# Fused attention and rational feed-forward kernel: which engine clamps the weight pieces and forms the remainder of g

## The chip, the cores and the metric

The kernel runs on one core of a Trainium2 chip. The metric is the device time of one execution in microseconds (us), as the median of several runs. The core's engines are TensorE (PE in the profile; PEld is its weight load), VectorE (DVE), ScalarE (ACT), GpSimd (POOL) and SyncE (SP), which issues most of the DMAs. Each engine works through its own list of instructions in order, and waits at the head of the list until the semaphores that the head needs are set.

## The reference, cut to what matters

An attention over 4 batches, 12 heads and 448 positions, with heads mixed before and after the softmax, gives x of 1792 rows and 768 columns. Then comes the feed-forward part, in which the change lies:

```python
def _moe_ref(x, w_in, w_out, a, b):
    h = x @ w_in
    h2 = h * h
    h3 = h2 * h
    P = a[0] + a[1] * h + a[2] * h2 + a[3] * h3
    Q = 1.0 + np.abs(b[0]) * np.abs(h) + np.abs(b[1]) * h2
    g = P / (Q + 1e-06)
    return (g @ w_out).astype(np.float32)
```

w_in is 768 x 2048 and w_out 2048 x 768. They reach the kernel as 64-bit floats, seen as pairs of 32-bit words.

## The kernel before, in words

**Arithmetic.** A matrix product of float32 accuracy is made from three products in a faster format: each operand is split into a head ("hi", rounded to the format) and a remainder ("lo", the value less its head), and head times head, head times remainder and remainder times head are summed in PSUM.

**Weights.** They come in 16 blocks f of 128 columns of w_in with the matching 128 rows of w_out, and each block in 4 pieces of 128 x 384, 64 pieces in all (`put_w`). A piece is loaded as word pairs (`load`, tile cr), its 64-bit floats are turned into 32-bit ones by bit operations, and then split. The steps of a piece in order: `mag` on ScalarE (absolute value of the upper words, tile cm), `clamp` on GpSimd (bounds the exponent, line 415), `shift`, `top` and `tail` on VectorE (lines 419, 424 and 430; tile cg), `hi` on ScalarE (tile w) and `lo` on GpSimd (line 446). 16 pieces (blocks 0 to 3) are made during the attention; they have an argument g. The other 48 are made during the feed-forward part, one beside each of its first 48 units.

**Units.** The feed-forward part has 64 units (`put_unit`): a unit is one block f for one batch of 448 rows. It has a first product of 18 matmuls into a bank of ps_s (`m1`, line 879), the rational function (ScalarE: lines 892, 895, 898, 902, 915 and 919; VectorE: `horner1` 905, `den2` 912, `horner2` 908, `step1` 922, `step2` 925, `quot` 929), the split of g into its head (`hi`, on ScalarE or VectorE, lines 236 and 238) and its remainder (`lo`, VectorE or GpSimd, line 939), and a second product of 6 times 3 matmuls into ps_t, ps_u and ps_a (`m2`, line 969). Four units make a turn: they add into the same six banks, which are then copied out (tile o, lines 236 and 238; in the last 16 units added to what is there, line 1006). ps_s has two banks, so the first product of a unit needs `horner2` of the unit two before it, the last reader of its bank.

**Order.** Nothing is ordered by the hardware's own choice: the program lists all steps with a planned duration, dependencies and a due time, and a planner (`Plan.run`) lays them on the engines and so fixes each engine's list. A step that may run on several engines goes where the plan has it first; the table `ON` names the engines. A change of an engine or of a planned duration thus changes the lists of all engines from there on.

```python
        a5 = add(copies(S, on=ON["g_hi"]), 0, hi, [d5, R["g"].take(), op_rest], at=at)
        d6 = add(subs(S, on=ON["g_lo"]), 0, lo, [a5], at=at)
```

Of the kernel before, what the change touches and what calls it, by code (L numbers as in the profile page):

```python
# [13 lines left out]
ALU = mybir.AluOpType  # L14
# [25 lines left out]
F64_MIN = 2.0 ** -15  # L40
F64_MAX = struct.unpack("f", struct.pack("I", 0x47EFF000))[0]
# [13 lines left out]
class Plan:  # L55
# [11 lines left out]
    def add(self, eng, dur, fn, deps=(), at=0.0, extra=0.0, since=0.0, after=(), mode=None, late=0.0):  # L67
        op = Op(eng, dur, fn, [d for d in deps if d is not None], at, extra, since, mode, late)
        op.behind = list(after)
        self.ops.append(op)  # L70
        return op
# [120 lines left out]
def act(n, sb=True):  # L192
    return 0.08 + 1.0e-3 * n + (0.05 if sb else 0.0)


def dve(n, fast=False):
    return 0.16 + 0.53e-3 * n if fast else 0.14 + 1.06e-3 * n
# [6 lines left out]
def copies(n, sb=True, on=("act", "dve")):  # L204
    return {e: act(n, sb) if e == "act" else dve(n, sb) for e in on}


def subs(n, on=("dve", "pool")):
    return {e: dve(n) if e == "dve" else pool(n) for e in on}
# [2 lines left out]
ON = {  # L212
    "q_hi": ('act', 'dve'), "q_lo": ("dve", "pool"), "k_hi": ('act', 'dve'), "k_lo": ('dve', 'pool'), "w_hi": ('act',), "w_lo": ("pool",),
    "s": ('act', 'dve'), "d_hi": ('act', 'dve'), "d_lo": ("dve", "pool"), "p": ("act", "dve"), "x_hi": ("act",),
    "g_hi": ("act", "dve"), "g_lo": ("dve", "pool"),
}


def dma(nbytes):
    return nbytes / 300e3  # L220
# [13 lines left out]
def move(nc, eng, o, i):  # L234
    if eng is nc.scalar:
        eng.copy(o, i)  # L236
    else:
        eng.tensor_copy(o, i)
# [3 lines left out]
def mixed_attention_then_rational_ffn(ctx: ExitStack, tc, q, k, v, w, wmix, mask, a, b2, out):  # L242
# [3 lines left out]
    nc = tc.nc  # L246
# [5 lines left out]
    add = plan.add  # L252
# [136 lines left out]
    def new_w(f):  # L389
        if f % CH == NR:  # L390
            W[f] = d_sb[1].rearrange("p n s -> p (n s)")[:, 0:2 * WC].rearrange("p (h c) -> p h c", h=2).bitcast(F32R)
        else:
            W[f] = sb["wr" if f % CH < NR else "wl"].tile([128, 2, WC], F32R, tag="w", name=f"w{f}")

    def room_w(f):
        return [R["d"].uses[NT - 1] if f % CH == NR else op_begin if f % CH < NR else op_rest]


    def put_w(f, c, at, since=0.0, g=None):
        sl = slice(c * CV, (c + 1) * CV)  # L400
        box = {}

        def load():
            t = sb["cr"].tile([128, CV, 2], I32, tag="cr", name="cr")
            nc.sync.dma_start(out=t.rearrange("p n t -> p (n t)"), in_=w[f, :, sl].bitcast(I32))
            box["hi"], box["lo"] = t[:, :, 1], t[:, :, 0]

        def mag():
            t = sb["cm"].tile([128, CV], I32, tag="cm", name="cm")
            nc.scalar.activation(t.bitcast(F32), box["hi"].bitcast(F32), AF.Abs)  # L410
            box["m"] = t

        def clamp():
            m = box["m"].bitcast(F32)
            nc.gpsimd.tensor_scalar(out=m, in0=m, scalar1=F64_MIN, scalar2=F64_MAX, op0=ALU.max, op1=ALU.min)  # L415

        def shift():
            m = box["m"]
            nc.vector.tensor_scalar(
                out=m, in0=m, scalar1=3, scalar2=0x3FFFFFFF, op0=ALU.logical_shift_left, op1=ALU.bitwise_and)  # L420

        def top():
            t = sb["cg"].tile([128, CV], I32, tag="cg", name="cg")
            nc.vector.scalar_tensor_tensor(  # L424
                out=t, in0=box["hi"], scalar=-0x40000000, in1=box["m"],
                op0=ALU.bitwise_and, op1=ALU.bitwise_or)
            box["g"] = t

        def tail():
            nc.vector.scalar_tensor_tensor(  # L430
                out=box["m"], in0=box["lo"], scalar=29, in1=box["g"],
                op0=ALU.logical_shift_right, op1=ALU.bitwise_or)

        def hi(eng):
            if f in VIA:
                t = sb["co"].tile([128, 2, CV], F32R, tag="co", name="co")
            else:
                if c == 0:
                    new_w(f)
                t = W[f][:, :, sl]  # L440
            move(nc, eng, t[:, 0, :], box["m"].bitcast(F32))
            box["o"] = t

        def lo(eng):
            t = box["o"]
            eng.tensor_sub(t[:, 1, :], box["m"].bitcast(F32), t[:, 0, :].bitcast(F32))  # L446

        def store():
            nc.sync.dma_start(out=w_scr[f][:, :, sl], in_=box["o"].bitcast(F32))

        ld = add("sp", 0.45, load, [R["cr"].take()], at=at - 5.0, extra=dma(128 * CV * 8), since=max(since, at - 9.0))
        near = lambda i, k: [] if g is None else [posts[min(g + i, len(groups) - 1)][k]]
        o1 = add("act", act(CV), mag, [ld, R["cm"].take(), *near(0, 3)], at=at, late=4.0)
        o2 = add("pool", 1.54, clamp, [o1, *near(0, 1)], at=at)
        o3 = add("dve", dve(CV, True), shift, [o2], at=at)
        o4 = add("dve", 0.59, top, [o3, R["cg"].take()], at=at)
        o5 = add("dve", 0.57, tail, [o4], at=at)
        R["cg"].uses[-1].append(o5)
        R["cr"].uses[-1].append(o5)
        if f in VIA:  # L460
            home = [R["co"].take()]
        elif c == 0:
            home = [*room_w(f), w_use[f - CH] if f >= CH else None]
        else:
            home = []
        o6 = add(copies(CV, on=ON["w_hi"]), 0, hi, [o5, *near(1, 3)] + [x for x in home if x], at=at, after=() if f in VIA else w_ld[f][:1])
        o7 = add(subs(CV, on=ON["w_lo"]), 0, lo, [o6, *near(1, 1)], at=at)
        R["cm"].uses[-1].append(o7)
        if f in VIA:
            o8 = add("sp", 0.57, store, [o7], at=at, extra=dma(128 * CV * 8), late=2.0)  # L470
            R["co"].uses[-1].append(o8)
            w_done[f].append(o8)
        else:
            w_ld[f].append(o6)
            w_ld[f].append(o7)
# [322 lines left out]
    for i in range(len(VIA) * NCV):  # L798
        g = first[1] + 6 + (first[NT - 1] - first[1] - 3) * i // (len(VIA) * NCV)
        put_w(VIA[i // NCV], i % NCV, at=tau[g], g=g)  # L800
# [247 lines left out]
    for f in range(PH):  # L1048
        if f not in VIA:
            for c in range(NCV):  # L1050
                put_w(f, c, at=END1 - 26.0 + 6.0 * c, since=END1 - 40.0 + 6.0 * c, g=len(groups) - 8 + 2 * c)
    for n in homes:
        put_load_x(n, at=END1 + UNIT * PH * (held.index(n) - 1) + 1 if n > 1 else END1 - 45.0)
    for u in range(len(units)):
        i = u + PH * NCV
        if i < NF * NCV:
            put_w(i // NCV, i % NCV, at=END1 + UNIT * u + 2.0, since=END1 + UNIT * u - 6.0)
        put_unit(u)
# [62 lines left out]
```

## Time and profile before

| | before |
|---|---|
| median of 3 runs | 840.03 us (836.45 to 842.73) |
| profiled execution | 838.34 us |
| its span, first to last instruction | 836.5 us |
| busy share of the span, PE / DVE / ACT / POOL | 96% / 81% / 60% / 43% |
| the chain that ended last, PE / DVE / ACT / DMA | 67% / 18% / 5% / 4% |
| mean granted clock of TensorE | 0.993 of full |

The times in the views are microseconds from the start of the span, unless marked ns. The busy share of an engine is the share of the stretch in which at least one of its instructions ran; two instructions that overlap count once. The feed-forward part's first product starts at 348.2 us, beside the end of the attention, and its last second product ends at 832 us. The chain that ended last follows the work back from the last instruction, at each step to what released it.

### The profile page before, as it was taken

The numbers are of one execution on the slowest core, as the hardware profiler recorded it, in microseconds if no ns is written. First come the engines' busy times: TensorE is split into PE (matmuls) and PEld (weight loads), VectorE is DVE, ScalarE is ACT, GpSimd is POOL, SyncE is SP. The second block draws the span as 40 slices with busy tenths as digits, with TensorE's granted clock in tenths as the row PEclk, the third lists the DMA queues.
The fourth block names the chain that finished last, engine by engine and source line by source line (L and its number), as shares of the span: only waits on it lengthen the run. The fifth ranks groups of instructions, "written<-read, shape, count | busy, mean of one in ns | idle before, by whom it ended". The sixth has DMA issues, their size and how long they took to land.

```text
span 836.5 us, 23297 instructions
## 1 busy us (share of the span) xinstructions
PE 802.2 (96%) x9360; PEld 597.8 (71%) x9360; DVE 677.4 (81%) x1158; ACT 501.5 (60%) x1098; POOL 358.4 (43%) x488
## 2 busy tenths in 40 slices
PE   5889999999999999999999999999999999999998
PEld 1244455554545454589989899998989999999997
DVE  5667788878878888789988898898898899676665
ACT  2456666646655666566677666665657676545542
POOL 2224444442444344634455545556646554312111
PEclk8899999999999999999999999999999999999999
DMA  6677888677886864984633265664476644366314
GB/s 201 217 202 224 249 264 271 198 218 253 257 229 199 258 217 143 358 298 174 230 123 101 79 217 135 200 139 100 79 236 164 159 112 67 61 226 241 115 62 155
DMA packets 71901, 155.46 MB, mean 186 GB/s; under 512 B 12561, under 2 KB 52337, under 8 KB 70641
## 3 DMA queue, kind: packets, MB, share of 16 engines
q1 hardware_dynamic: 67736, 141.99, 52.2%
q0 software_dynamic: 3456, 11.01, 8.1%
q8 instruction: 74, 1.21, 0.6%
q10 hardware_dynamic: 600, 0.97, 0.4%
q14 instruction: 35, 0.28, 0.1%
HBM read 77.49 MB, written 37.75 MB: 138 GB/s over the span
## 4 chain that ended last, share of the span: by engine, by line
PE 67%; DVE 18%; ACT 5%; DMA 4%; issue 4%; POOL 1%; SPq 1%; ACTq 0%; DVEq 0%; POOLq 0%
PE ps_s L879 18%; PE ps_s L496 8%; PE ps_a L640 7%; PE ps_u L969 7%; PE ps_t L969 7%; PE ps_a L969 6%; PE ps_t L565 4%; PE ps_u L565 4%; PE ps_u L705 3%; DVE cg L424 2%; PE ps_t L705 2%; DMA kk<-in_k 2%; DVE nm L571 2%; ACT e L580 2%; DVE cm L430 2%
## 5 line engine op out<-in xcount | busy, mean ns | idle before, releaser
L415 POOL TENSOR_SCALAR cm<-cm 128x384 f32<-128x384 f32 x64 | 103.0, 1612 | 43.6 <-ACT cm L410 43.1
L656 DVE STREAM_TRANSPOSE aa<-ps_a 128x448 f32<-128x448 f32 (+1 forms) x184 | 107.8, 618 | 12.1 <-PE ps_a L640 11.4
L939 POOL TENSOR_TENSOR g<-ua,g 128x448 fp32r<-128x448 f32 x47 | 57.4, 1221 | 128.3 <-ACT g L236 72.7
L600 POOL TENSOR_SCALAR krs<-kpost,rr 128x64 f32<-128x64 f32 x180 | 81.6, 466 | 70.9 <-DVE rr L591 50.0
L879 PE MATMUL ps_s<-xs,w 128*128 128x448 f32 x504 | 107.5, 366 | 2.7 <-DVE m L908 2.6
L879 PE MATMUL ps_s<-d,w 128*128 128x448 f32 x504 | 107.6, 367 | 2.0 <-DVE m L908 1.9
L496 PE MATMUL ps_s<-kk,q 64*64 64x448 f32 x720 | 95.2, 556 | 9.4 <-DMA kk<-in_k 5.1
L879 PEld LDWEIGHTS ps_s<-xs,w 128*128 128x128 f32 x504 | 94.3, 188 | 12.0 <-DVE m L908 4.2
L879 PEld LDWEIGHTS ps_s<-d,w 128*128 128x128 f32 x504 | 94.1, 188 | 11.6 <-DVE m L908 3.1
L236 ACT COPY st<-ps_s 120x448 f32<-120x448 f32 (+1 forms) x120 | 60.2, 533 | 68.9 <-PE ps_s L496 35.0
L640 PEld LDWEIGHTS ps_a<-e,krs 64*32 64x32 f32 x2880 | 44.7, 106 | 74.2 <-issue 31.5
L640 PE MATMUL ps_a<-e,krs 64*32 64x224 f32 x2880 | 92.3, 355 | 1.6 <-DVE aa L656 0.6
L892 ACT ACTIVATE m<-ps_s,a_sb 128x448 f32<-128x448 f32 x64 | 46.1, 720 | 66.7 <-PE ps_s L879 64.0
L969 PE MATMUL ps_u<-g,w 128*128 128x448 f32 x336 | 83.9, 366 | 0.0
L969 PE MATMUL ps_a<-g,w 128*128 128x448 f32 x336 | 83.8, 366 | 0.0
L969 PE MATMUL ps_t<-g,w 128*128 128x448 f32 x336 | 83.4, 366 | 0.0
L446 POOL TENSOR_TENSOR w<-cm,w 128x384 fp32r<-128x384 f32 x48 | 55.7, 1160 | 62.8 <-ACT w L236 62.8
L587 POOL TENSOR_SCALAR sm<-sm 128x2 f32<-128x2 f32 (+1 forms) x92 | 20.6, 224 | 124.1 <-ACT e L580 122.2
L580 ACT ACTIVATE e<-ps_t,nm 128x448 f32<-128x448 f32 x92 | 57.7, 634 | 24.7 <-DVE nm L571 16.7
L580 ACT ACTIVATE e<-ps_u,nm 128x448 f32<-128x448 f32 x88 | 55.2, 633 | 21.9 <-DVE nm L571 18.7
L969 PEld LDWEIGHTS ps_t<-g,w 128*128 128x128 f32 x336 | 63.0, 188 | 5.5 <-DVE g L939 0.3
L969 PEld LDWEIGHTS ps_u<-g,w 128*128 128x128 f32 x336 | 63.1, 188 | 5.2
(90 smaller groups left out, 1514.9 us busy)
## 6 DMA issues: line engine op xcount, KB each, us to landing
d<-st SPq DMA_DIRECT2D x144, 210.0 KB
cr<-in_w SPq DMA_DIRECT2D x64, 384.0 KB
d<-x_scr SPq DMA_DIRECT2D x5, 2688.0 KB
xs<-x_scr SPq DMA_DIRECT2D x4, 2688.0 KB
o_scr<-o POOLq DMA_DIRECT2D x24, 448.0 KB, 6.0
d<-st SPq DMA_DIRECT2D x42, 157.5 KB
x_scr<-xs SPq DMA_DIRECT2D x12, 540.0 KB
q<-in_q SPq DMA_DIRECT2D x16, 384.0 KB
```

Of the source, the lines that this page charges most:

```text
L236: eng.copy(o, i)
L415: nc.gpsimd.tensor_scalar(out=m, in0=m, scalar1=F64_MIN, scalar2=F64_MAX, op0=ALU.max, op1=ALU.min)
L446: eng.tensor_sub(t[:, 1, :], box["m"].bitcast(F32), t[:, 0, :].bitcast(F32))
L496: nc.tensor.matmul(box["s"][hh][i0:i1, 0:S], lhsT=Q[T][d, pr, i0:i1], rhs=K[b][d, pr, :], start=True, stop=True)
L565: nc.tensor.matmul(box[r if nt == 2 else 0]["t"][64 * c:64 * c + 64, 0:S], lhsT=kpre[p], rhs=Dt[T][p, kb + c if nt == 2 else kb, :], start ...
L580: nc.scalar.activation(e, box[r]["t"][:, 0:S], AF.Exp, bias=box[0]["nm"][:, r:r + 1], accum_out=box[0]["sm"][:, r:r + 1])
L600: eng.tensor_scalar_mul(box[r]["kr"], kpost, rr)
L640: nc.tensor.matmul(banks[c]["p"][q_:q_ + BT, JH * r:JH * (r + 1)], lhsT=box[r]["kr"][p, m_, :], rhs=box[r]["e"][p, JH * jh:JH * (jh + 1)], ...
L656: nc.vector.transpose(o, src)
L879: nc.tensor.matmul(h[:, 0:S], lhsT=W[fi][:, wi, kk * 128:(kk + 1) * 128], rhs=x[:, kk // 3, xj, kk % 3, :], start=(n == 0), stop=(n == 3 * ...
L939: eng.tensor_sub(g[:, 1, :], box["rc"], g[:, 0, :].bitcast(F32))
L969: nc.tensor.matmul(O[key][:, 0:S], lhsT=W[fi][:, wi, DM + m * 128:DM + (m + 1) * 128], rhs=box["g"][:, gi, :], start=(f == 0 and n == 0), ...
```

## The change

For the 48 pieces of the feed-forward part the clamp is issued on VectorE, with a planned 0.32 us, and on GpSimd as before for the 16 pieces that are made in the attention. The remainder of g is VectorE's alone. The remainder of the weights stays on GpSimd.

```diff
@@ -212,7 +212,7 @@
-    "g_hi": ("act", "dve"), "g_lo": ("dve", "pool"),
+    "g_hi": ("act", "dve"), "g_lo": ("dve",),
@@ -410,9 +410,9 @@
-        def clamp():
+        def clamp(eng):
             m = box["m"].bitcast(F32)
-            nc.gpsimd.tensor_scalar(out=m, in0=m, scalar1=F64_MIN, scalar2=F64_MAX, op0=ALU.max, op1=ALU.min)
+            eng.tensor_scalar(out=m, in0=m, scalar1=F64_MIN, scalar2=F64_MAX, op0=ALU.max, op1=ALU.min)
@@ -451,7 +451,7 @@
-        o2 = add("pool", 1.54, clamp, [o1, *near(0, 1)], at=at)
+        o2 = add({"dve": 0.32} if g is None else {"pool": 1.54}, 0, clamp, [o1, *near(0, 1)], at=at)
```

The lists change from the first unit's end on (some 370 us). On VectorE 48 clamps come in, and the remainders of g there rise from 17 to 64; the planner also moves 4 heads of g to VectorE (28 before, 32 now) and 5 copies of o away from it (43 before, 38 now). VectorE's list at the same place of the program, from `step1` (L922) of one unit to `horner2` (L908) of the next, the 15th of the 64. Before:

```order
L922 TENSOR_TENSOR sq<-sq,ua 128x448
L419 TENSOR_SCALAR cm<-cm 128x384
L925 SCALAR_TENSOR_TENSOR ua<-sq,ua 128x448
L424 SCALAR_TENSOR_TENSOR cg<-cr,cm 128x384
L929 SCALAR_TENSOR_TENSOR ua<-m,a_sb,ua 128x448
L430 SCALAR_TENSOR_TENSOR cm<-cr,cg 128x384
L238 COPY o<-ps_a 128x448
L419 TENSOR_SCALAR cm<-cm 128x384
L424 SCALAR_TENSOR_TENSOR cg<-cr,cm 128x384
L905 TENSOR_TENSOR m<-m,ps_s 128x448
L430 SCALAR_TENSOR_TENSOR cm<-cr,cg 128x384
L908 SCALAR_TENSOR_TENSOR m<-m,a_sb,ps_s 128x448
```

VectorE's list at that place now:

```order
L922 TENSOR_TENSOR sq<-sq,ua 128x448
L415 TENSOR_SCALAR cm<-cm 128x384
L925 SCALAR_TENSOR_TENSOR ua<-sq,ua 128x448
L419 TENSOR_SCALAR cm<-cm 128x384
L929 SCALAR_TENSOR_TENSOR ua<-m,a_sb,ua 128x448
L424 SCALAR_TENSOR_TENSOR cg<-cr,cm 128x384
L238 COPY o<-ps_a 128x448
L939 TENSOR_TENSOR g<-ua,g 128x448
L430 SCALAR_TENSOR_TENSOR cm<-cr,cg 128x384
L905 TENSOR_TENSOR m<-m,ps_s 128x448
L912 TENSOR_TENSOR sq<-sq,ua 128x448
L908 SCALAR_TENSOR_TENSOR m<-m,a_sb,ps_s 128x448
```

Ahead of `horner2` stand now a clamp (L415), a remainder of g (L939) and `den2` (L912); a second piece's shift, top and tail have gone behind it. One or two units later the list goes from `den2` (L912) of one unit to its `step1` (L922) so, before:

```order
L905 TENSOR_TENSOR m<-m,ps_s 128x448
L912 TENSOR_TENSOR sq<-sq,ua 128x448
L908 SCALAR_TENSOR_TENSOR m<-m,a_sb,ps_s 128x448
L922 TENSOR_TENSOR sq<-sq,ua 128x448
L925 SCALAR_TENSOR_TENSOR ua<-sq,ua 128x448
L419 TENSOR_SCALAR cm<-cm 128x384
```

and now:

```order
L908 SCALAR_TENSOR_TENSOR m<-m,a_sb,ps_s 128x448
L912 TENSOR_TENSOR sq<-sq,ua 128x448
L939 TENSOR_TENSOR g<-ua,g 128x448
L415 TENSOR_SCALAR cm<-cm 128x384
L419 TENSOR_SCALAR cm<-cm 128x384
L424 SCALAR_TENSOR_TENSOR cg<-cr,cm 128x384
L922 TENSOR_TENSOR sq<-sq,ua 128x448
```

Between `den2` and `step1`, where VectorE waits for two steps of ScalarE (L915, L919), stood one instruction, and now stand four. GpSimd's list in the feed-forward part, some rows before:

```order
L446 TENSOR_TENSOR w_7296<-cm,w_7296 128x384
L415 TENSOR_SCALAR cm<-cm 128x384
L939 TENSOR_TENSOR g<-ua,g 128x448
L415 TENSOR_SCALAR cm<-cm 128x384
L446 TENSOR_TENSOR w_7296<-cm,w_7296 128x384
L939 TENSOR_TENSOR g<-ua,g 128x448
L446 TENSOR_TENSOR w_7296<-cm,w_7296 128x384
```

and at the same place now:

```order
L446 TENSOR_TENSOR w_7034<-cm,w_7034 128x384 x4
L446 TENSOR_TENSOR w_7309<-cm,w_7309 128x384 x4
L446 TENSOR_TENSOR w_7527<-cm,w_7527 128x384 x4
L446 TENSOR_TENSOR w_7791<-cm,w_7791 128x384 x4
L1020 DMA o_scr_128<-o 128x896 x2
L446 TENSOR_TENSOR w_8146<-cm,w_8146 128x384 x2
```

Nothing but the remainders of the weights (four per block) and the 24 adding DMAs of the partial outputs is left there.

## Rows read from the trace of the kernel before

**Rows 1.** Busy time by engine, attention left out (stretch, us; PE, PEld, DVE, ACT, POOL; clock):

```profile
390.00:700.00 310.00, 305.34 (x1494) 279.52 (x1493) 276.32 (x450) 204.07 (x388) 172.13 (x136) 1.00 0.53 147
700.00:832.00 132.00, 132.00 (x653) 122.23 (x652) 91.11 (x150) 66.49 (x117) 27.60 (x24) 1.00 0.42 134
```

**Rows 2.** Timeline of PE: first products that open a turn (start, us, ..., idle before):

```profile
433.24 3.94 PE L879 MATMUL ps_s<-xs,w 128*128 128x448 f32 x18 [1.56 <-DVE m L908]
463.44 3.97 PE L879 MATMUL ps_s<-xs,w 128*128 128x448 f32 x18 [0.58 <-DVE m L908]
...
583.20 3.95 PE L879 MATMUL ps_s<-d,w 128*128 128x448 f32 x18 [1.94 <-DVE m L908]
...
730.84 3.81 PE L879 MATMUL ps_s<-d,w 128*128 128x448 f32 x18
...
760.02 3.81 PE L879 MATMUL ps_s<-xs,w 128*128 128x448 f32 x18
```

**Rows 3.** Groups on DVE, 390 to 700 us (busy us, mean ns | idle before):

```profile
L424 DVE SCALAR_TENSOR_TENSOR cg<-cr,cm 128x384 int32<-128x384 int32 x44 | 33.2, 755 | 0.7
...
L925 DVE SCALAR_TENSOR_TENSOR ua<-sq,ua 128x448 f32<-128x448 f32 x42 | 32.1, 765 | 1.0 <-DVE sq L922 0.5
L922 DVE TENSOR_TENSOR sq<-sq,ua 128x448 f32<-128x448 f32 x42 | 28.4, 675 | 12.9 <-ACT ua L919 12.3
...
L430 DVE SCALAR_TENSOR_TENSOR cm<-cr,cg 128x384 int32<-128x384 int32 x43 | 27.7, 644 | 0.4
...
L905 DVE TENSOR_TENSOR m<-m,ps_s 128x448 f32<-128x448 f32 x41 | 25.2, 614 | 6.2 <-ACT ua L898 6.1
L419 DVE TENSOR_SCALAR cm<-cm 128x384 int32<-128x384 int32 x44 | 24.7, 560 | 2.9 <-POOL cm L415 2.6
...
L238 DVE CAST g<-ua 128x448 fp32r<-128x448 f32 x15 | 9.4, 624 | 1.2
```

**Rows 4.** The same lines, 390 to 700 us, durations in ns: least/median/most:

```profile
L424 DVE SCALAR_TENSOR_TENSOR cg<-cr,cm x44: 543/558/2259, 397.5 to 700.0; 128x384 int32<-128x384 int32 x44
L925 DVE SCALAR_TENSOR_TENSOR ua<-sq,ua x42: 610/624/1965, 392.4 to 693.4; 128x448 f32<-128x448 f32 x42
L430 DVE SCALAR_TENSOR_TENSOR cm<-cr,cg x43: 543/551/1411, 398.2 to 693.9; 128x384 int32<-128x384 int32 x43
L905 DVE TENSOR_TENSOR m<-m,ps_s x41: 604/614/622, 401.5 to 698.0; 128x448 f32<-128x448 f32 x41
L419 DVE TENSOR_SCALAR cm<-cm x44: 346/360/1291, 396.3 to 698.6; 128x384 int32<-128x384 int32 x44
L238 DVE CAST g<-ua x15: 379/395/1200, 414.6 to 695.2; 128x448 fp32r<-128x448 f32 x15
```

**Rows 5.** Groups on POOL, 390 to 700 us:

```profile
L415 POOL TENSOR_SCALAR cm<-cm 128x384 f32<-128x384 f32 x44 | 72.2, 1643 | 31.4 <-ACT cm L410 31.0
L446 POOL TENSOR_TENSOR w<-cm,w 128x384 fp32r<-128x384 f32 x40 | 47.0, 1175 | 50.3 <-ACT w L236 50.3
L939 POOL TENSOR_TENSOR g<-ua,g 128x448 fp32r<-128x448 f32 x28 | 34.3, 1224 | 43.1 <-ACT g L236 25.4 <-DVE g L238 17.7
```

**Rows 6.** Timeline of DVE ahead of three of these first products:

```profile
431.30 1.29 DVE L419 TENSOR_SCALAR cm<-cm 128x384 int32<-128x384 int32 x1
...
459.24 1.26 DVE L419 TENSOR_SCALAR cm<-cm 128x384 int32<-128x384 int32 x1
...
461.71 0.61 DVE L905 TENSOR_TENSOR m<-m,ps_s 128x448 f32<-128x448 f32 x1
462.24 0.55 DVE L430 SCALAR_TENSOR_TENSOR cm<-cr,cg 128x384 int32<-128x384 int32 x1
...
579.79 1.17 DVE L419 TENSOR_SCALAR cm<-cm 128x384 int32<-128x384 int32 x1
```

**Rows 7.** Timeline of POOL at the same three places:

```profile
430.99 1.38 POOL L939 TENSOR_TENSOR g<-ua,g 128x448 fp32r<-128x448 f32 x1 [0.18 <-ACT g L236]
...
459.12 1.16 POOL L939 TENSOR_TENSOR g<-ua,g 128x448 fp32r<-128x448 f32 x1 [1.64 <-ACT g L236]
...
579.48 1.26 POOL L446 TENSOR_TENSOR d<-cm,d 128x384 fp32r<-128x384 f32 x1 [1.71 <-ACT d L236]
```

## The prediction

> **What bounds the kernel now.** I read the busy times by stretch first, then the few idle gaps of the bounding engine, then the groups and durations of the engine that it waits for. From 390 to 700 us, where weight pieces are made beside the units, TensorE is busy 305.34 of 310 us and VectorE 276.32; after 700 us TensorE is busy for all of 132 us and VectorE for 91.11 [rows 1]. So TensorE sets the time, and a change of the other engines can win only what TensorE loses to them. To size that loss, take the starts of the first products that open a turn. Undisturbed, a turn takes 760.02 - 730.84 = 29.18 us. From 433.24 to 730.84 there are ten turns in 297.60 us where 291.8 would do: 5.8 us lost, and 1.56 us more stand as idle just before 433.24 [rows 2]. Together 7.4 us can be won at most, which puts the best case at 838.3 - 7.4 = 830.9 us in terms of the profiled execution. All the gaps in the rows have one releaser: `horner2` on VectorE (L908), the last reader of the ps_s bank [rows 2]. VectorE comes late there although it idles for 310 - 276.3 = 33.7 us of the stretch.
>
> Why it is late shows in its durations. `shift` has a median of 360 ns and a mean of 560, `top` 558 and 755, `tail` 551 and 644, `step2` 624 and 765, the cast of g 395 and 624; `horner1`, which reads PSUM, has 614 and 614 [rows 3, 4]. The long cases lie beside GpSimd instructions: ahead of three of the gaps a `shift` took 1.29, 1.26 and 1.17 us, each while GpSimd ran a remainder, two of g and one of a weight piece [rows 6, 7]. Mean less median times count gives the stall: `top` 44 x 0.197 = 8.7, `shift` 44 x 0.200 = 8.8, `step2` 42 x 0.141 = 5.9, `tail` 43 x 0.093 = 4.0, the cast 15 x 0.229 = 3.4; in all **30.8 us**.
>
> **The change part by part**, for 390 to 700 us.
>
> Added work on VectorE. The clamp: 44 pieces. The trace has no clamp on VectorE; the nearest row is `shift`, the same engine, operation, shape and element size, at 0.36 us median; the other end is `top` at 0.558, which reads two tiles [rows 4]. I take 0.36, the same operation: 44 x 0.36 = 15.8 us (24.6 at the other end). The remainder of g: 28 go over [rows 5]. The pitch of such instructions back to back is 462.24 - 461.71 = 0.53 us [rows 6], so 28 x 0.53 = 14.8 us. The planner's shifts (4 more casts at 0.395, 5 fewer copies of o at about 0.53, in 64 units, of which 42 lie here): -0.7 us. Sum: **+29.9 us**.
>
> Stalls removed. Of GpSimd's 44 clamps, 44 remainders of weights (40 in the row, 4 more into tile d) and 28 remainders of g [rows 5], 72 of 116 go. By count, 30.8 x 72 / 116 = 19.1 us of stall would go; at worst none does, because the remainders of weights alone hold VectorE up as often as before. Of the three long shifts two stood beside what goes and one beside what stays [rows 6, 7]; I take half: **-15.4 us**. VectorE's busy time becomes 276.3 + 29.9 - 15.4 = 290.8 us, where TensorE's own work of the stretch needs 310 - 7.4 = 302.6. It fits, but only if the waits of VectorE shrink from 33.7 us: at 19.2 us there is no change, at 11.8 all of the loss is won.
>
> Waits. 12.3 us stand before `step1`, for ScalarE's logarithm and exponential, and 2.6 before `shift`, for the clamp [rows 3]. The second goes with GpSimd's clamp. The first goes where the new lists put a remainder, a clamp and a shift between `den2` and `step1`: three instructions of 0.53, 0.36 and 0.36 us cover about the two steps of ScalarE. Leaves 33.7 - 14.9 = 18.8 us. Of the 6.1 us that `horner1` waits for ScalarE's `mag` of the unit [rows 3], I take half as gone, because a VectorE with more to do comes there later: 15.7 us left. 290.8 + 15.7 = 306.5 us, 3.5 less than 310.
>
> New waits. On VectorE the clamp waits for ScalarE's absolute value, the remainder for ScalarE's head of g, and behind them in the list stand `horner1` and `horner2`, on which TensorE's next first product hangs. On GpSimd these waits were 31.0 and 25.4 us [rows 5], but GpSimd, 172 of 310 us busy [rows 1], came early to both. I price them at nothing in the sum, because the lists put other work between; the other end is in the second rival.
>
> Where it would show: at the place before the 15th unit's `horner2` the list has gained a clamp, a remainder and a `den2` (0.36 + 0.53 + 0.53) and lost a shift, top and tail (0.36 + 0.56 + 0.55), so the way to `horner2` is as long as it was, less the stalls. Half of these gone is half of 7.4 us, 3.7: the second way to the same number. After 700 us 17 remainders at 0.53, 9 us, go to an engine with 41 us to spare, beside a TensorE that is never idle: nothing. The attention up to 370 us keeps its lists: nothing. The forecast is **3.5 us less**.
>
> The Trainium skill, page "SBUF — State Buffer", section "Who interferes with whom", says that VectorE and GpSimd share one pair of ports under an exclusive lock, that a VectorE instruction with two inputs in SBUF, or a single-input one at double rate, competes for it, and that the later one blocks until the other has finished; one with a single SBUF input at normal rate does not compete. `horner1` agrees with its 614 against 614 [rows 4]. By that rule the moves are no free trade: the clamp and the remainder are two more instructions that can be blocked.
>
> **The rivals.**
>
> *Nothing comes of it.* The waits before `step1` are filled but others keep their size: 290.8 + 18.8 = 309.6, a difference of 0.4 us, about 840 by the median; and with the clamp at 0.56 us it is 318.4 and some 9 us more, 849. For it: VectorE at 290.8 of 302.6 is 96% full, and an engine that works in order rarely does without waits. Against: the waits are its own idleness while TensorE is ahead.
>
> *VectorE becomes the bound.* The place is the whole stretch with pieces: GpSimd's remainders of weights go on blocking it as long in sum as the three kinds did, since a fuller VectorE meets each of them. Then nothing is removed: 276.3 + 29.9 = 306.2, and with 15.7 of waits 321.9 us, 11.9 more for 44 of the 48 pieces, 13 for all: 851 in the profiled terms, 853 by the median. It decides from the point at which work and waits pass 310 us. For it: the third shift [rows 6, 7]. Against: the two others, and that GpSimd's computing time falls from 154 us or more to about a third [rows 5].
>
> *Each remainder blocks VectorE for its whole length.* 44 x 1.175 = 51.7 us of stall in place of 30.8: 276.3 - 30.8 + 51.7 + 29.9 + 15.7 = 342.8 us, 36 us more over 48 pieces, about 876. The trace speaks against it: 116 instructions with 154 us or more [rows 5] gave 30.8 us, a fifth. This is what the lock on the Trainium skill's page named above would do in full; by that rule VectorE would have to be caught at the start of every one.
>
> *All is won.* No gap is left: 7.4 us, 832.6 by the median. Nothing beyond it can be won, since TensorE's work is unchanged. That the change might not do what it says is excluded: the lists show 48 clamps and all 64 remainders on VectorE.
>
> **How the numbers follow.** The profiled execution took 838.3 us, 1.7 below the median of 840.0, and the runs spread over 6 us; I count from the median: 840.0 - 3.5 = 836.5. Chances: forecast, 833 to 839, 0.44; nothing, 839 to 848, 0.28; VectorE the bound 0.15 and whole blocks 0.03, above 848; all won, below 833, 0.10. A measurement of this kernel tells about 1%, 8.4 us, from no change. Only the last case with some luck of the runs passes 831.6: faster 0.08. Slower by more (above 848.4) are the two bound cases: 0.18. The rest, 0.74, is within. The range leaves out some 0.05 below 831 and 0.15 above 850.
>
> **What would show it.** Right: VectorE's clamp at about 0.36 us; VectorE busy about 94% of the stretch with pieces; its means of `shift` and `top` nearer to their medians; `step1`'s wait for ScalarE mostly gone; turns at 29.2 to 29.4 us. Wrong: turns of 30 us or more with TensorE waiting for `horner2` in each; a clamp of 0.56 us; long waits of the clamp or the remainder for ScalarE; remainders of weights beside stalls of 1 us on VectorE as often as before.

## The result and the profile after

The changed kernel takes 832.25 us in the median of 10 runs (827.66 to 836.85), the kernel before 839.58 us (835.37 to 846.02): a ratio of 0.9911, with a 95% interval of 0.9887 to 0.9936. That is some 7.5 us less by the ratio, where 3.5 were forecast and 7.4 was the most that was thought to be had; the interval allows 5.4 to 9.5. The profiled execution took 830.89 us, with a span of 829.1. From the start of the first first product to the end of the last second product it took 477.7 us (347.46 to 825.14), where the profiled execution before took 484.4 (348.17 to 832.54). So 6.7 of the 7.4 us between the two profiled executions lie in the feed-forward part.

The busy times by stretch, as in [rows 1] (PE, PEld, DVE, ACT, POOL, clock, DMA share, GB/s):

```profile
390.00:700.00 310.00, 310.00 (x1526) 286.03 (x1525) 291.81 (x531) 213.30 (x405) 67.17 (x65) 1.00 0.53 147
```

TensorE had 4.66 us without work in this stretch before; it has none now. VectorE's busy time went up by 15.5 us, to 291.81, and GpSimd's down by 105. First products in the timeline of PE, as in [rows 2], one of before first; all but those of 427.25 and 424.52 open a turn (start and length, us; a gap ahead would stand in brackets at the end):

```profile
427.25 3.81 PE L879 MATMUL ps_s<-d 128*128 128x448 f32 x18
```

In the changed kernel:

```profile
424.52 3.81 PE L879 MATMUL ps_s<-d 128*128 128x448 f32 x18
436.12 3.84 PE L879 MATMUL ps_s<-xs,w 128*128 128x448 f32 x18
...
459.96 3.82 PE L879 MATMUL ps_s<-xs,w 128*128 128x448 f32 x18
...
489.24 3.81 PE L879 MATMUL ps_s<-d,w 128*128 128x448 f32 x18
...
723.45 3.81 PE L879 MATMUL ps_s<-d,w 128*128 128x448 f32 x18
...
752.62 3.81 PE L879 MATMUL ps_s<-xs,w 128*128 128x448 f32 x18
```

From 459.96 to 723.45 there are nine turns, 29.28 us each, against 29.76 in the ten turns before and 29.17 for a turn without pieces (723.45 to 752.62). A turn without gaps thus takes 0.1 us more where pieces are made than where none are, which the prediction's 7.4 us, worked out with 29.18, left out. Every gap ahead of a first product is gone. Also the early part, where TensorE's lists differ most, has none: the pair of close first products whose second one waited 1.56 us (427.25 and 433.24 [rows 2]) is now 11.6 us apart (424.52 and 436.12).

VectorE by groups in that stretch, as in [rows 3] (busy us, mean ns | idle before and its releaser):

```profile
L929 DVE SCALAR_TENSOR_TENSOR ua<-m,a_sb,ua 128x448 f32<-128x448 f32 x43 | 36.8, 857 | 0.4
L922 DVE TENSOR_TENSOR sq<-sq,ua 128x448 f32<-128x448 f32 x44 | 29.4, 667 | 5.0 <-ACT ua L919 4.7
...
L925 DVE SCALAR_TENSOR_TENSOR ua<-sq,ua 128x448 f32<-128x448 f32 x44 | 27.2, 619 | 0.3
L939 DVE TENSOR_TENSOR g<-ua,g 128x448 fp32r<-128x448 f32 x43 | 26.5, 617 | 0.6 <-ACT g L236 0.2
L905 DVE TENSOR_TENSOR m<-m,ps_s 128x448 f32<-128x448 f32 x43 | 26.4, 614 | 0.0
L424 DVE SCALAR_TENSOR_TENSOR cg<-cr,cm 128x384 int32<-128x384 int32 x44 | 26.4, 599 | 0.8
L430 DVE SCALAR_TENSOR_TENSOR cm<-cr,cg 128x384 int32<-128x384 int32 x43 | 24.5, 570 | 0.0
L419 DVE TENSOR_SCALAR cm<-cm 128x384 int32<-128x384 int32 x44 | 18.4, 418 | 0.8
L415 DVE TENSOR_SCALAR cm<-cm 128x384 f32<-128x384 f32 x44 | 17.4, 395 | 0.0
L238 DVE CAST g<-ua 128x448 fp32r<-128x448 f32 x18 | 12.6, 698 | 1.2
...
L238 DVE COPY o<-ps_t 128x448 f32<-128x448 f32 x15 | 9.3, 622 | 8.8 <-PE ps_t L969 8.8
```

`quot` (L929) in the kernel before, in the same view and in that of durations (least/median/most, ns):

```profile
L929 DVE SCALAR_TENSOR_TENSOR ua<-m,a_sb,ua 128x448 f32<-128x448 f32 x42 | 32.2, 767 | 0.5
```

```profile
L929 DVE SCALAR_TENSOR_TENSOR ua<-m,a_sb,ua x42: 670/680/1322, 393.5 to 694.4; 128x448 f32<-128x448 f32 x42
```

`top` (L424) went from a mean of 755 to 599 ns, `shift` (L419) from 560 to 418, `tail` (L430) from 644 to 570, `step2` (L925) from 765 to 619; `quot` went the other way, from 767 to 857. The wait ahead of `step1` (L922) fell from 12.3 to 4.7 us, that of `horner1` (L905) from 6.1 to nothing, and what waits most on VectorE now are the copies out of ps_t, for TensorE (8.8 us): VectorE is ahead of TensorE there.

The clamp in the view of durations (least/median/most, ns), and the neighbours of one in the timeline of VectorE:

```profile
L415 DVE TENSOR_SCALAR cm<-cm x44: 346/353/1178, 395.2 to 698.3; 128x384 f32<-128x384 f32 x44
```

```profile
453.02 0.35 DVE L415 TENSOR_SCALAR cm<-cm 128x384 f32<-128x384 f32 x1
453.29 0.62 DVE L925 SCALAR_TENSOR_TENSOR ua<-sq,ua 128x448 f32<-128x448 f32 x1
...
464.98 0.35 DVE L415 TENSOR_SCALAR cm<-cm 128x384 f32<-128x384 f32 x1
465.36 0.36 DVE L419 TENSOR_SCALAR cm<-cm 128x384 int32<-128x384 int32 x1
```

Its median is 353 ns, as `shift` had let expect; at 453.02 it takes up 0.27 us of VectorE's time, since the next instruction does not need its result, and at 464.98, where the next one does, 0.38.

### The profile page after: what moved, and what is told of

It reads as the page before. It is cut to its first block, busy times and chain, and to the rows that moved or that the text cites. A ratio compares the mean times of both kernels' runs of the same rounds, so it can differ in the third digit from the quotient of the medians.

```text
span 829.1 us, 23254 instructions
## 1 busy us (share of the span) xinstructions
PE 801.0 (97%) x9360; PEld 598.0 (72%) x9360; DVE 690.6 (83%) x1252; ACT 502.4 (61%) x1099; POOL 222.2 (27%) x393
## 4 chain that ended last, share of the span: by engine, by line
PE 84%; DMA 6%; DVE 5%; ACT 2%; issue 1%; POOL 0%; SPq 0%; ACTq 0%; DVEq 0%; POOLq 0%
PE ps_s L879 28%; PE ps_u L969 9%; PE ps_t L969 9%; PE ps_a L969 9%; PE ps_s L496 8%; PE ps_a L640 7%; PE ps_t L565 4%; PE ps_u L565 4%; DMA d<-st 4%; PE ps_u L705 2%; PE ps_t L705 2%; DVE nm L571 2%; ACT e L580 2%; DMA kk<-in_k 1%; DVE aa L656 1%
## 5 line engine op out<-in xcount | busy, mean ns | idle before, releaser
L656 DVE STREAM_TRANSPOSE aa<-ps_a 128x448 f32<-128x448 f32 (+1 forms) x184 | 107.8, 618 | 11.6 <-PE ps_a L640 10.8
L446 POOL TENSOR_TENSOR w<-cm,w 128x384 fp32r<-128x384 f32 x48 | 53.7, 1118 | 177.8 <-ACT w L236 168.4
L969 PEld LDWEIGHTS ps_a<-g,w 128*128 128x128 f32 x336 | 63.1, 188 | 5.2
L496 PEld LDWEIGHTS ps_s<-kk,q 64*64 64x64 f32 x720 | 29.5, 135 | 49.4 <-issue 21.5
L915 ACT ACTIVATE ua<-sq 128x448 f32<-128x448 f32 x64 | 37.1, 580 | 33.6 <-DVE sq L912 33.4
```

Of the source, the lines that this page charges most:

```text
L496: nc.tensor.matmul(box["s"][hh][i0:i1, 0:S], lhsT=Q[T][d, pr, i0:i1], rhs=K[b][d, pr, :], start=True, stop=True)
L656: nc.vector.transpose(o, src)
L915: nc.scalar.activation(box["ua"], box["vv"], AF.Ln)
L969: nc.tensor.matmul(O[key][:, 0:S], lhsT=W[fi][:, wi, DM + m * 128:DM + (m + 1) * 128], rhs=box["g"][:, gi, :], start=(f == 0 and n == 0), ...
```

## The experiments

Theory 1 is the prediction's: GpSimd's instructions stall VectorE, and with fewer of them `horner2` comes in time. Theory 2: the planner's new lists do it, whatever stalls there are. Theory 3: a piece's way through GpSimd's clamp, 1.6 us, is what held VectorE's list up. All ratios are to the kernel before, which was run again beside each set of experiments (medians 838.57 and 839.14 us), with 95% intervals; the changed kernel's is 0.9911. **Stall** means here what an instruction of VectorE took above the median of its group, summed over 390 to 700 us of the profiled execution: 39.0 us before, 24.6 in the changed kernel. Every instruction with more than 0.15 us of it (68 before, 40 in the changed kernel) overlaps a computing instruction of GpSimd, although GpSimd computes in half of the stretch before and in a sixth of it in the changed kernel; each is put down to the one that it overlaps most.

**The clamp alone.**

```diff
-    "g_hi": ("act", "dve"), "g_lo": ("dve",),
+    "g_hi": ("act", "dve"), "g_lo": ("dve", "pool"),
```

> The clamp of the 48 pieces is VectorE's as in the changed kernel; the remainder of g may go to either engine, and the planner puts 59 of 64 on GpSimd. Theory 1 (GpSimd's instructions stall VectorE, and fewer of them let horner2 come in time): 48 GpSimd instructions go and 12 come, against 72 to 95 that went in the change; the clamp's were the ones with the weakest stalls, so part of the gain: 834 to 837 us. Theory 2 (the planner's new lists make the gain, not the stalls): its lists differ from both kernels, and the list of TensorE holds one early pair of first products with only one group between, as before had; anything from 832 to 840. Theory 3 (the way of a piece through GpSimd's clamp of 1.6 us is what made VectorE late): all of the gain, 832.

Measured: 837.97 us, 1.0004 (0.9982 to 1.0027): nothing. Theory 3 falls with it. Theory 1 had expected a part of the gain, 834 to 837 us, and missed; theory 2 had allowed anything from 832 to 840. What theory 1 had left out is that the clamp on VectorE is stalled itself. VectorE and GpSimd by groups in this kernel, 390 to 700 us:

```profile
L415 DVE TENSOR_SCALAR cm<-cm 128x384 f32<-128x384 f32 x43 | 30.6, 712 | 0.0
```

```profile
L939 POOL TENSOR_TENSOR g<-ua,g 128x448 fp32r<-128x448 f32 x37 | 46.8, 1265 | 61.2 <-ACT g L236 27.7 <-DVE g L238 24.3 <-issue 9.3
```

With GpSimd free of clamps the planner gives it more remainders of g (59 of 64 in place of 47), and now the moved clamp is what is caught: a mean of 712 ns for an instruction with a median of 353 in the changed kernel, some 15 us over the stretch. The stalls of all groups come to 44.8 us, above the 39.0 of before, with 80 computing instructions of GpSimd in place of 116. TensorE waits for `horner2` as before (busy 306.05 of 310 us).

**The remainder alone.**

```diff
-        o2 = add({"dve": 0.32} if g is None else {"pool": 1.54}, 0, clamp, [o1, *near(0, 1)], at=at)
+        o2 = add({"pool": 1.54}, 0, clamp, [o1, *near(0, 1)], at=at)
```

> The remainder of g is VectorE's alone as in the changed kernel; all 64 clamps stay on GpSimd. Theory 1 (stalls by GpSimd): 47 GpSimd instructions with strong stalls go, at 47 x 0.53 us more work on VectorE: about half of the gain, 834 to 838 us. Theory 2 (the lists): anything from 832 to 840. Theory 3 (the way of a piece through the clamp): nothing gained, 839 to 841.

Measured: 834.49 us, 0.9947 (0.9915 to 0.9978): a good half of the gain, within theory 1's range and far from theory 3's; theory 2 had allowed it too. Its stalls come to 29.1 us. Its busy times show TensorE nearly without gaps, and the largest left in its timeline is of the old kind:

```profile
390.00:700.00 310.00, 309.47 (x1515) 283.72 (x1514) 290.16 (x484) 208.57 (x395) 143.92 (x109) 1.00 0.52 147
```

```profile
462.86 3.97 PE L879 MATMUL ps_s<-xs,w 128*128 128x448 f32 x18 [0.43 <-DVE m L908]
```

**The changed lists, with GpSimd's work put back as spare work.** The plan does not know of it, so the lists of TensorE, VectorE, ScalarE and SyncE are those of the changed kernel; in the trace those of the first three have the same instructions in the same order.

```diff
             eng.tensor_scalar(out=m, in0=m, scalar1=F64_MIN, scalar2=F64_MAX, op0=ALU.max, op1=ALU.min)
+            if eng is nc.vector:
+                nc.gpsimd.tensor_scalar(
+                    out=spare[:, 0:CV], in0=box["hi"].bitcast(F32), scalar1=F64_MIN, scalar2=F64_MAX, op0=ALU.max, op1=ALU.min)
...
             eng.tensor_sub(g[:, 1, :], box["rc"], g[:, 0, :].bitcast(F32))
+            if u % 4 < 3:
+                nc.gpsimd.tensor_sub(spare, g[:, 0, :].bitcast(F32), g[:, 0, :].bitcast(F32))
```

> The changed kernel with the same lists on TensorE, VectorE, ScalarE and SyncE, and GpSimd given spare instructions of the size of those that it lost: beside each of the 48 clamps one of the same form from the loaded words into a spare tile, and for 48 of the 64 units a subtraction of two reads of g's head into the spare tile. Nobody waits for their result. Theory 1 (stalls by GpSimd): VectorE's busy time in the feed-forward part rises by 15 us or more, TensorE waits for horner2 again, and as VectorE also keeps the added work, the time is at or above that of before: 838 to 850 us. Theory 2 (the lists) and theory 3 (the piece's way): the time of the changed kernel, 832 to 834.

Measured: 853.65 us, 1.0175 (1.0133 to 1.0218), above the top of theory 1's range and far from the other two. Instructions whose results nobody reads cost some 22 us against the changed kernel; from 390 to 700 us no wait of TensorE, VectorE or ScalarE in the trace ends with an instruction of GpSimd. Busy times, and three of the gaps in TensorE's timeline:

```profile
390.00:700.00 310.00, 297.97 (x1432) 271.72 (x1432) 301.01 (x499) 199.02 (x376) 165.81 (x131) 0.98 0.51 143
```

```profile
530.85 5.47 PE L883 MATMUL ps_s<-xs,w 128*128 128x448 f32 x18 [1.83 <-DVE m L912]
...
563.36 3.93 PE L883 MATMUL ps_s<-d,w 128*128 128x448 f32 x18 [1.50 <-DVE m L912]
...
686.00 5.42 PE L883 MATMUL ps_s<-xs,w 128*128 128x448 f32 x18 [2.11 <-DVE m L912]
```

(L912 is `horner2` in this file.) Some of these first products take 5.4 us in place of 3.9, and the stretch's granted clock is 0.98 of full, where it was 1.00. Over the first product at 530.85 it is 0.69:

```profile
530.85:536.32 5.47, 5.47 (x19) 4.96 (x20) 5.44 (x10) 3.51 (x7) 2.63 (x3) 0.69 0.95 393
```

So after some of the gaps TensorE ran part of a first product at the lower of its two levels (1.2 in place of 2.4 GHz). The gaps and what follows them count together.

**The old lists, with GpSimd's instructions cut short.** The lists are those of the kernel before, in the trace too. The kernel leaves out most of each clamp and of each remainder of g that GpSimd makes.

```diff
+            if g is None:
+                m = m[:, 0:8]
             nc.gpsimd.tensor_scalar(out=m, in0=m, scalar1=F64_MIN, scalar2=F64_MAX, op0=ALU.max, op1=ALU.min)
...
+            box["short"] = eng is nc.gpsimd
+            n = 8 if box["short"] else S
-            eng.tensor_sub(g[:, 1, :], box["rc"], g[:, 0, :].bitcast(F32))
+            eng.tensor_sub(g[:, 1, 0:n], box["rc"][:, 0:n], g[:, 0, 0:n].bitcast(F32))
...
-                        O[key][:, 0:S], lhsT=W[fi][:, wi, DM + m * 128:DM + (m + 1) * 128], rhs=box["g"][:, gi, :],
+                        O[key][:, 0:S], lhsT=W[fi][:, wi, DM + m * 128:DM + (m + 1) * 128], rhs=box["g"][:, 0 if box["short"] else gi, :],
```

> The kernel before with the same lists, but GpSimd's clamp of the 48 pieces of the feed-forward part does only 8 of 384 columns, and its remainder of g only 8 of 448, where the second product then reads the head twice: this leaves out part of the computation. Theory 1 (stalls by GpSimd): VectorE loses the stalls without the added work, means of its instructions fall to their medians, the gaps ahead of a turn's first product go: 831 to 834 us. Theory 2 (the lists): the time of before, 838 to 841. Theory 3 (the piece's way through the clamp): also faster here, 832 to 835, so that this run tells theory 2 from the others only.

Measured: 831.71 us, 0.9913 (0.9883 to 0.9944): the whole gain with the old lists. Theory 2 falls. Busy times:

```profile
390.00:700.00 310.00, 310.00 (x1526) 286.03 (x1525) 263.43 (x455) 210.11 (x400) 92.29 (x139) 1.00 0.53 147
```

VectorE does the same instructions as before in 263.43 us in place of 276.32, for more of TensorE's work, and TensorE has no gap. The same 41 units, from the 7th first product to the 48th, compare so, before and here:

```profile
393.59:696.71 303.12, 298.46 (x1459) 273.15 (x1458) 269.69 (x437) 199.61 (x381) 170.77 (x135) 1.00 0.53 146
```

```profile
395.76:692.37 296.61, 296.61 (x1459) 273.64 (x1458) 251.63 (x437) 199.22 (x380) 89.25 (x135) 1.00 0.54 150
```

The stalls fell by 17 us, to 22.1: none is left beside what was cut short, and those beside the remainders of the weights, which still run in full, are as large as before (22.5 us, 22.6 before). The close pair of first products, which the old lists still have, does not cost anything either, once these stalls are gone:

```profile
429.42 3.81 PE L881 MATMUL ps_s<-d 128*128 128x448 f32 x18
...
433.68 3.83 PE L881 MATMUL ps_s<-xs,w 128*128 128x448 f32 x18
```

And a VectorE with 28 us less to do than in the changed kernel makes it no faster: both are at TensorE's own time, 477.7 us from the first first product to the end of the last second product in either profiled execution. Here a piece's way through the clamp is short too, so that this run alone does not speak against theory 3; the first two do.

**How far VectorE is from being the bound.** Each of the 48 clamps on VectorE is issued twice, and in a second kernel three times (`range(2)` here, `range(3)` there, on VectorE only):

```diff
-            eng.tensor_scalar(out=m, in0=m, scalar1=F64_MIN, scalar2=F64_MAX, op0=ALU.max, op1=ALU.min)
+            for _ in range(1 if eng is nc.gpsimd else 2):
+                eng.tensor_scalar(out=m, in0=m, scalar1=F64_MIN, scalar2=F64_MAX, op0=ALU.max, op1=ALU.min)
```

> The changed kernel with each of VectorE's 48 clamps issued twice; the lists are otherwise the same. 44 x 0.36 = 15.8 us more work on VectorE from 390 to 700 us, where it is busy 291.8 and waits 18.2 us. Theory A (the waits left are VectorE's idleness ahead of TensorE, and give way): nearly all is taken up, 832 to 836 us. Theory B (the waits left are owed to ScalarE and TensorE and stay, so VectorE is already at its bound): 15.8 x 48 / 44 = 17 us on top, 846 to 850 us.

> The changed kernel with each of VectorE's 48 clamps issued three times: 31.7 us more work on VectorE from 390 to 700 us. Theory A (the waits left give way): 291.8 + 31.7 = 323.5 us, 13.5 over the stretch, 15 over 48 pieces, and some waits: 846 to 852 us. Theory B (they stay): 35 us on top, 864 to 868 us.

Measured: 837.85 us, 0.9982 (0.9958 to 1.0005) with two, and 858.03 us, 1.0215 (1.0145 to 1.0285) with three. Both fall between the theories. Against the changed kernel the first 17 us of added work (48 x 0.36) cost 0.71%, 6 us, and the next 17 cost 2.3%, some 20 us. The lists are otherwise the same, so the 41 units from the 7th first product to the 48th can be set side by side, with one clamp, with two and with three:

```profile
387.82:689.31 301.49, 301.49 (x1483) 278.15 (x1482) 282.51 (x513) 205.50 (x389) 65.18 (x63) 1.00 0.53 149
```

```profile
390.10:696.57 306.47, 303.46 (x1483) 277.57 (x1482) 293.46 (x554) 205.44 (x388) 63.14 (x62) 1.00 0.52 146
```

```profile
394.00:716.29 322.29, 307.71 (x1483) 279.93 (x1482) 308.55 (x597) 205.72 (x388) 63.46 (x62) 0.99 0.50 139
```

VectorE is busy 282.5, 293.5 and 308.6 us and idle for 19.0, 13.0 and 13.7. The first set of clamps adds 11.0 us of busy time: 6.0 come out of the idle time and 5.0 lengthen the stretch. The second set adds 15.1 us, and the idle time gives no more. So only some 6 of the 19 us of waits give way: theory A holds for a third of them, theory B for the rest. In the second kernel the gaps are back at nearly every turn:

```profile
503.91 3.91 PE L880 MATMUL ps_s<-d,w 128*128 128x448 f32 x18 [2.38 <-DVE m L909]
...
565.50 3.91 PE L880 MATMUL ps_s<-d,w 128*128 128x448 f32 x18 [2.23 <-DVE m L909]
...
597.38 5.49 PE L880 MATMUL ps_s<-d,w 128*128 128x448 f32 x18 [2.43 <-DVE m L909]
```

From 390 to 700 us VectorE is busy 296.53 of 310 us there. Some 13 us of idleness in 310 stay even where it is plainly what TensorE waits for.

**Which of GpSimd's instructions stalls.** The spare work of the third experiment in its two halves: the 48 clamps alone, and the 48 subtractions alone.

> The changed kernel with only the 48 spare GpSimd instructions that have the clamp's form (one tile in, 1.7 us long). Theory 1 with every GpSimd instruction alike: some 0.35 us of stall each, 17 us, within VectorE's 18 us of waits: 833 to 838 us. Theory 1 with the stall by the length: 1.7 us against 1.15, more than in the run with the spare subtractions alone: 838 to 845 us. If the one-input form hardly stalls VectorE, as its share of the stalls in the trace of before would have it: 831 to 833 us.

> The changed kernel with only the 48 spare GpSimd subtractions (two tiles in, 1.15 us long). With every GpSimd instruction alike: the same as the run with the spare clamps, 833 to 838 us. With the stall by the length: less than that run, 832 to 836. If it is the two-input form that stalls VectorE: most of what both together cost, 840 to 850 us, and more than the run with the spare clamps.

Measured: 836.23 us, 0.9977 (0.9948 to 1.0006), with the spare clamps, 836.49 us, 0.9975 (0.9946 to 1.0004), with the spare subtractions. The two are alike in time, although a spare clamp is 1.84 us long, and a spare subtraction 1.14:

```profile
L418 POOL TENSOR_SCALAR spare<-cr 128x384 f32<-128x384 f32 x43 | 79.2, 1842 | 3.6 <-DMA cr<-in_w 3.4
```

```profile
L942 POOL TENSOR_TENSOR spare<-g 128x448 f32<-128x448 f32 x32 | 36.5, 1142 | 61.3 <-ACT g L236 31.4 <-DVE g L238 26.8 <-PE ps_t L972 3.0
```

In time the runs fit "every GpSimd instruction alike"; the stalls do not. Taken above the changed kernel's medians, in one profiled execution each, the 43 spare clamps of the stretch make 14.1 us of stalls and the 32 spare subtractions 14.2, that is 0.33 and 0.44 us each: the shorter instruction stalls more. The sums, and with them the times, come out alike because the stretch holds more of the clamps.

Each half costs some 5.5 us and both together 22 us. In the same 41 units as above VectorE is busy 11 and 12 us more with one half and 28 us more with both, and its idle time falls from 19.0 us to 12.1, 11.0 and 9.5: as with the clamps on VectorE, most of the first half of the load comes out of its waits, and little of the second:

```profile
387.60:693.12 305.52, 302.71 (x1483) 277.80 (x1482) 293.38 (x513) 205.38 (x389) 138.35 (x104) 1.00 0.52 147
```

```profile
392.39:697.83 305.44, 303.04 (x1483) 277.56 (x1482) 294.47 (x513) 206.09 (x390) 99.61 (x94) 1.00 0.52 147
```

```profile
391.67:712.00 320.33, 308.30 (x1483) 281.26 (x1482) 310.85 (x515) 206.08 (x390) 170.26 (x137) 0.98 0.51 140
```

The spare clamps run when their words arrive, not when the real ones did, so a price per instruction in the old kernel does not follow from this.

## Why the prediction was right, and where its size was off

**What bounds.** Right. TensorE set the time, all it lost was lost at `horner2`, and that loss was the whole of what could be won: the two kernels without gaps (the changed one and the old lists with short GpSimd instructions) stand at 832.25 and 831.71. That 7.4 was forecast for it and 7.5 measured is closer than either number is sure: the interval of the measured one is 5.4 to 9.5, and the feed-forward part of the profiled executions became 6.7 us shorter.

**Why VectorE was late.** Right, and shown by runs that leave the lists as they are: taking GpSimd's time away wins all, giving it back loses more than all.

**The clamp at 0.36 us.** Right: 0.353 in the median.

**The stalls.** Sized rightly in sum, in part by luck. Mean less median times count over the five groups of the prediction falls from 30.8 to about 11 us, but `quot`, which it did not count, rises from 3.7 to 7.4, and the clamp adds 1.8 of its own; over all of VectorE's instructions I work out 39 us before and 25 after, a fall of 14 for the forecast 15.4. The forecast was half of 30.8 us. By the GpSimd instruction that each stalled one overlaps most, the 39.0 us were 6.9 beside the 44 clamps, 9.5 beside the 28 remainders of g and 22.6 beside the 44 remainders of the weights, which stay. The moved instructions, 62% by count, thus made 16.4 us or 42% of the stalls, and the remainders of the weights make 24.5 us now, 1.9 more. Half of a base that left out 8 us came near the real fall, somewhat over a third of the whole.

**The added work was over-sized.** This is one half of the error. The stretch now holds all of TensorE's 310 us, where it held 302.6 before; VectorE's 291.8 us are therefore 284.8 for the work of before, not 290.8. With the stalls about right, the added work was some 23 us, not 29.9. A small part of that is traced: a clamp was priced at its duration, but takes 0.27 us where its follower is independent; counted from its start to its end or to the next start, whichever comes first, the 44 clamps add 13.9 us besides their stalls, where 15.8 was forecast. The copies of o that went to ScalarE (35 on VectorE in the stretch, where it had 39) had been counted nearly in full. Where the other 5 us went no row shows.

**The waits.** For the same work they fell from 33.7 to 17.8 us, forecast 15.7. The two that were named went as said or nearly: 12.3 to 4.7 ahead of `step1`, 2.6 to nothing for the clamp, and the 6.1 of `horner1` to nothing, not to half. The copies' wait for TensorE grew by 2.5 us. The step that failed is "290.8 + 15.7 = 306.5 us, 3.5 less than 310": with the added work of 23 us it would have come out at about 300, below TensorE's 302.6, so all of the loss would have been the forecast. The second way, "half of these gone is half of 7.4 us", failed in taking the loss as proportional to the stalls. Over the kernels with stalls of 22, 25, 29, 39 and 45 us (short instructions, changed kernel, remainder alone, before, clamp alone) TensorE's idle time in the stretch is 0, 0, 0.5, 4.7 and 4.0 us. That fits a slack at `horner2` that must be used up before a gap arises; the slack itself was not measured.

**The new waits.** Priced at nothing, rightly: the remainder waits 0.2 us for ScalarE's head of g, the clamp not at all.

**The rivals.** "VectorE becomes the bound" did not come, but it was near: 17 us more work costs 6 us, and 34 us cost 26. The forecast's point, that no change of time comes at 19.2 us of waits and the full gain at 11.8, was too strict, since it took VectorE's work too high: the full gain came at 17.8 us of waits. "Each remainder blocks for its whole length" is excluded by the changed kernel: 44 weights' remainders of 1.15 us would be 50 us of stalls, and all stalls are 25. "VectorE becomes the bound" had one thing right: the remainders of the weights go on stalling VectorE (24.5 us after 22.6), but they did not take over what the other instructions had caused.

## What to carry to other kernels

Compare mean and median of each instruction of the engine that the bounding engine waits for: where they part for operands in SBUF and not for those in PSUM, as here, see whether the long ones lie beside another engine's instructions. Those cost time even where nobody reads their results, and neither their number nor their length alone gave the cost: 0.16 us for each of GpSimd's clamps before, 0.34 for each remainder of g, 0.51 for each remainder of a weight piece, which were the ones that stayed. Moving work from GpSimd onto a VectorE that was 89% busy won, since the moved instructions were two to four times shorter there (means of 0.62 against 1.22 us and of 0.395 against 1.64) and took their stalls with them; moving the clamp alone let the planner refill GpSimd, and won nothing. Before such a move issue the work to be added twice: how the engine's idle time answers tells how much of it is really to be had, here some 6 of 19 us.

## What the runs showed of the hardware that was not expected

A moved instruction can itself become the one that is stalled: VectorE's clamp has a mean of 395 ns in the changed kernel, and of 712 beside a GpSimd with 59 remainders of g. How a stalled instruction ends differs by what stalls it. In the changed kernel all 40 of VectorE's long instructions lie beside two-input remainders of GpSimd, and each ends as if it had begun, at the median length of its group, 0.13 to 0.21 us ahead of the remainder's end, for example a `quot` beside a remainder:

```profile
468.29 1.02 POOL L446 TENSOR_TENSOR w<-cm,w 128x384 fp32r<-128x384 f32 x1 [5.39 <-ACT w L236]
```

```profile
468.32 1.47 DVE L929 SCALAR_TENSOR_TENSOR ua<-m,a_sb,ua 128x448 f32<-128x448 f32 x1
```

The 48 beside remainders in the kernel before do the same (0.13 to 0.20 us), but the 20 beside its one-input clamps go on more than 1.1 us ahead of the clamp's end, of 1.5 to 2.1 us that a clamp takes there. So a remainder held VectorE up until nearly its end and a clamp only through a part of it, which fits the smaller price of the clamp; the ends of GpSimd's instructions in a profile are rough, so the offsets are good to tell the two apart and no more.

And TensorE's gaps of 1.8 us or more were followed in some cases by a first product of 5.4 to 5.5 us in place of 3.9 (the spare-work kernel at 530.85 and 686.00, the three-clamp kernel at 597.38), with a granted clock of 0.69 to 0.70 over these products and of 0.98 and 0.99 over the stretch; gaps of 1.5 us and less in the same rows were not, and gaps of 2.38 and 2.23 us were not either, so the gap's length alone does not decide it.
